# Token-mixing layer: a sixth pair of output tiles by seven products, with a sum and the residual additions done by accumulating DMAs

## The chip, the core and the metric

One Trainium2 chip, one core. Its engines run side by side, each in its own order of instructions: TensorE (PE in the profile, its weight loads PEld), VectorE (DVE), ScalarE (ACT), GpSimd (POOL) and SyncE (SP), which here only issues DMAs. POOL issues DMAs too, those that add to their destination. The metric is the device time of one execution in microseconds, lower is better; the kernel is compared by the median of its runs.

## What is computed

x is 2048 tokens by 448 channels. The first half of the layer is a linear attention block, the second a token-mixing MLP. Both add to x; six vectors (sa, ca, ga, sb, cb, gb) come from c and w_mod.

```
x = x + ga * A(layernorm(x) * (1 + ca) + sa)
h = layernorm(x) * (1 + cb) + sb
u = gelu(einsum("bsd,sf->bdf", layernorm(h), w1) + b1)     # S = 2048 -> F = 1792, across tokens
y = einsum("bdf,fs->bds", u, w2) + b2                      # F = 1792 -> S = 2048
out = x + gb * transpose(y)
```

The change lies in the last two lines: the product of u (14 row tiles of 128 by 448) with w2 (1792 by 2048), which gives 16 output tiles of 128 tokens by 448 channels, and the sum with x. The factor gb is multiplied into u, and gb * b2 is added to x beforehand (L1059).

## The kernel before, in words

**Precision.** Every 32-bit operand of a product is split into a high part that TensorE takes (written by ACT, L76) and a remainder (written by DVE, L77). A product of two split operands is three matmuls of 448 columns (`acc3`, L739 to L742): high by high, and the two mixed ones.

**Two ways to one result.** In the last stage the 16 output tiles come out of PSUM in two ways. *Plain* tiles (10 to 15 before the change): for each of 14 row tiles f of w2, `load1` fetches it, `split1` splits it, `mult1` runs three matmuls of 448 columns per output tile. One plain piece is one f, for one or two output tiles: 10 with 11, 12 with 13, then 14 and 15 alone. *Blocks* (tiles 0 to 9): two output tiles make a block q, whose part of w2 is a 2 by 2 arrangement of quarters a11, a12, a21, a22. It is multiplied by Strassen's scheme as Winograd arranged it: seven products instead of eight, of quarters or of sums of quarters. `PRODS` (L901) lists them with the sum that is made after each split: s1 = a21 + a22, s2 = s1 - a11, s3 = a11 - a21, s4 = a12 - s2. `split7` splits one factor (two pieces of 512 and 384 columns) and makes the sum with `sub` on DVE (L896). `mult7` runs one product: seven pairs of a matmul of 448 columns (L928, high part) and one of 224 (L929, remainder). The factors that come from u (`b..`, `t..`) are made once by `finish_u`.

**Out of the blocks.** `out7` runs after each product. It copies PSUM to SBUF on ACT (`copy2`, L934) and adds on DVE (`out2`: L938 of 448 columns, then two halves of 224 into x, L939 and L940; the last product adds twice straight from PSUM, L962 and L963). The finished tile of x is stored by SP (`store`, L943).

**x in between.** While w1 is being multiplied, DVE adds gb * b2 to each tile of x (L1059) and SP parks all 16 tiles in DRAM (`xpark`, L1060). The last stage fetches each back ahead of its use (`fetch_x`, L1043). The SBUF tiles of this stage all come from one pool of 76 slots; a load waits until the slot that it takes over is free.

**Order.** The order of PE's work is written out by hand: `order` is 8 plain pieces, then the products of all blocks in turn with the other plain pieces spread evenly between them, then 10 plain pieces. The loop at L1072 takes one entry at a time: loads are issued up to 12 entries ahead (`load2`, with all eight loads of a block at its first product), splits up to 4 entries ahead (`split2`), then the product and its output. Each engine runs its share of this in program order, as soon as what it waits for is there.

**The end.** For the last plain tile the last LAST = 3 pieces are held back: `mult_last` (L986) adds what is there to x, then multiplies these pieces for the first CUT = 336 columns, adds (L998) and stores (L999) them, and does the same for the other 112.

POOL issues accumulating DMAs earlier in the kernel (L244, L376, L399, L405: SBUF into SBUF), and none in this stage.

Of the kernel before, what the change touches and what calls it, by code (L numbers as in the profile page):

```python
# [8 lines left out]
F32 = mybir.dt.float32  # L9
F32R = mybir.dt.float32r  # L10
AF = mybir.ActivationFunctionType
ALU = mybir.AluOpType
AX = mybir.AxisListType

P = 128
S, D, F = 2048, 448, 1792
NT = S // P
NF = F // P
# [9 lines left out]
DVE_LOW = (0, 1, 13, 14, 15)  # L28
AHEAD = 8
LAG = 5  # L30
LAST, CUT = 3, 336
MOD_AT = {11: [(4, 0)], 12: [(4, 1)], 13: [(4, 2)], 14: [(4, 3)], 15: [(3, 0), (3, 1)]}
QS = {0: 2, 4: 2}
WARM = 12
# [10 lines left out]
def block_kernel(ctx: ExitStack, tc: tile.TileContext, x, wqkv, wo, w1, b1, w2, b2, c, wmod, out):  # L45
    nc = tc.nc
    xf = x.flatten_outer_dims()
    of = out.flatten_outer_dims()
# [4 lines left out]
    park = ctx.enter_context(tc.tile_pool(name="park", bufs=1, space=bass.MemoryType.DRAM))  # L53
# [8 lines left out]
    def slot(name, w=D, dt=F32, parts=P):  # L62
        return slots.tile([parts, w], dt, name=name, tag="slot", padded_shape=[P, 512])

    def tslot(name, dt=F32, parts=P, w=D):
        return tok.tile([parts, w], dt, name=name, tag="tok", padded_shape=[P, 512])
# [5 lines left out]
    def bank(name):  # L72
        return psum.tile([P, 512], F32, name=name, tag="bank")
# [26 lines left out]
    X = [None] * NT  # L100
# [123 lines left out]
    def load_to(i):  # L224
        while done["load"] < min(i, len(pieces)):
            k = done["load"]
            src, r, c0, n = pieces[k]
            raws[k] = slot(f"pr{k}", n * P)
            nc.sync.dma_start(raws[k], src[r * P:(r + 1) * P, c0 * P:(c0 + n) * P])
            done["load"] += 1  # L230

    def split_to(i):
        while done["split"] < min(i, len(pieces)):
            k = done["split"]
            n = pieces[k][3]
            if k in TOKP:
                hi, lo = tslot(f"ph{k}", F32R, w=n * P), tslot(f"pl{k}", F32R, w=n * P)
            else:
                hi, lo = slot(f"ph{k}", n * P, F32R), slot(f"pl{k}", n * P, F32R)
            if k in PIECE_DMA:  # L240
                full = raws.pop(k)
                nc.scalar.activation(hi, full, AF.Copy)
                nc.scalar.activation(lo, hi.bitcast(F32), AF.Copy, scale=-1.0)
                nc.gpsimd.dma_start(lo, full, accum_op=ALU.add)  # L244
            else:
                split(raws.pop(k), hi, lo)
            parts[k] = (hi, lo)
            done["split"] += 1
# [287 lines left out]
    for t in range(3, NT):  # L536
# [38 lines left out]
        if t == 4:  # L575
            for g in range(4):
                w = tslot(f"wo{g}", parts=G)
# [48 lines left out]
    for ch in range(4):  # L626
        for g in range(4):
            s = slice(g * G, (g + 1) * G)
# [133 lines left out]
    for i in range(NT + LAG):  # L762
# [13 lines left out]
        t = i - LAG  # L776
# [54 lines left out]
    uparts = ctx.enter_context(tc.tile_pool(name="uparts", bufs=1, reuse_waits="tile"))  # L831
    HD = D // 2
    PAIRS, RS = NF // 2, ((0, 4), (4, 3))
    NS7 = 5
    uw, uops, ufull = {}, {}, {}

    def u_parts(r, name, src):
# [39 lines left out]


    w2v = w2.rearrange("(r e p) c -> e p r c", e=2, p=P)
    raw2, hilo, acc2, cop = {}, {}, {}, {}  # L880
    QUADS = {"a11": (0, 0), "a12": (1, 0), "a21": (0, 1), "a22": (1, 1)}

    def load_quads(q):
        for name, (fo, to) in QUADS.items():
            raw2[q, name] = []
            for r0, n in RS:
# [2 lines left out]
                nc.sync.dma_start(w.rearrange("p (r c) -> p r c", c=P), w2v[fo, :, r0:r0 + n, c0:c0 + P])  # L889
                raw2[q, name].append(w)  # L890

    def sub(q, out, a, b, op=ALU.subtract, into=None):
        res = []
        for i, (r0, n) in enumerate(RS):
            w = raw2[q, into][i] if into else slot(f"{out}_{q}_{r0}", n * P)
            nc.vector.tensor_tensor(w, raw2[q, a][i], raw2[q, b][i], op=op)  # L896
            res.append(w)
        raw2[q, out] = res


    PRODS = (("a11", "b11", 0, ("s1", "a21", "a22", ALU.add)), ("a12", "b21", 1, ("s2", "s1", "a11")),  # L901
             ("s2", "t2", 0, ("s3", "a11", "a21", ALU.subtract, "a21")),
             ("s1", "t1", 2, ("s4", "a12", "s2", ALU.subtract, "a12")), ("s3", "t3", 0, None),
             ("s4", "b22", 2, None), ("a22", "t4", 0, None))

    def split7(q, m):
        a, _, _, add = PRODS[m]
        hilo[q, m] = []
        for w, (r0, nr) in zip(raw2[q, a], RS):
            h, l = slot(f"{a}h_{q}_{r0}", nr * P, F32R), slot(f"{a}l_{q}_{r0}", nr * P, F32R)  # L910
            split(w, h, l)
            hilo[q, m].append((h, l))
        if add:
            sub(q, *add)

    def mult7(q, m):
        a, b, k, _ = PRODS[m]
        opens = m in (0, 1, 3)
        if opens:
            acc2[q, k] = bank(f"y{q}_{k}")  # L920
        ps = acc2[q, k]
        closes = m in (1, 5, 6)
        cut = hilo.pop((q, m))
        for r in range(PAIRS):
            (h, l), i = cut[r // 4], r % 4
            w, wh = uops[b, r]
            s = slice(i * P, (i + 1) * P)
            nc.tensor.matmul(ps[:, :D], h[:, s], w, start=opens and r == 0, stop=False, skip_group_check=True)  # L928
            nc.tensor.matmul(ps[:, :HD], l[:, s], wh, start=False, stop=closes and r == PAIRS - 1,  # L929
                             skip_group_check=True)  # L930

    def copy2(q, k, name):
        cop[q, name] = slot(f"c{name}_{q}")
        nc.scalar.activation(cop[q, name], acc2[q, k][:, :D], AF.Copy)  # L934

    def out2(q, k, name, t, half):
        c, x = cop.pop((q, name)), X[t][:, half * HD:(half + 1) * HD]
        nc.vector.tensor_add(c, acc2[q, k][:, :D], c)  # L938
        nc.vector.tensor_add(x, x, c[:, :HD])  # L939
        nc.vector.tensor_add(x, x, c[:, HD:])  # L940

    def store(t):
        nc.sync.dma_start(of[t * P:(t + 1) * P, :], X[t])  # L943

    def out7(q, m):
        t0, t1 = 2 * q, 2 * q + 1
        if m == 0:
            copy2(q, 0, "c1")
        elif m == 1:
            out2(q, 1, "c1", t0, 0)  # L950
        elif m == 2:
            copy2(q, 0, "c2")
        elif m == 3:
            copy2(q, 2, "c5")
        elif m == 4:
            out2(q, 0, "c5", t1, 1)
        elif m == 5:
            out2(q, 2, "c2", t0, 1)
            store(t0)
        else:  # L960
            x = X[t1][:, :HD]
            nc.vector.tensor_add(x, acc2[q, 0][:, :HD], x)  # L962
            nc.vector.tensor_add(x, acc2[q, 0][:, HD:D], x)  # L963
            store(t1)


    def load1(t, n, f):
# [39 lines left out]


    sevens = [(q, m) for q in range(NS7) for m in range(7)]
    plains = [(t, n, f) for t, n in ((10, 2), (12, 2), (14, 1), (15, 1)) for f in range(NF)]  # L1010
    LEAD, TAIL = 8, 10
    order = [("p", p) for p in plains[:LEAD]]
    mid = plains[LEAD:len(plains) - TAIL]
# [21 lines left out]
    k = NT  # L1035
    jobs = [j for f in range(4) for j in finish_u(f, accs[f])]

    xleft = list(range(NT))
    xpark = [park.tile([P, D], F32, name=f"xpark{t}") for t in range(NT)]

    def fetch_x(t):
        X[t] = slot(f"xb{t}")
        nc.sync.dma_start(X[t], xpark[t])  # L1043

    k += LAG - 1
    for o0, n in W1G[1:]:
        if early:
            accs, first = early, LAG - 1
            early = None
        else:  # L1050
            accs, first = [bank(f"up{o0 + i}") for i in range(n)], 0
        for r in range(first, NT):
            load_to(k + AHEAD)
            split_to(k + 3)
            if jobs:
                jobs.pop(0)()
            if xleft and k % 2:
                t = xleft.pop(0)
                nc.vector.scalar_tensor_tensor(X[t], mods[5], b2c[:, t:t + 1], X[t], op0=ALU.mult, op1=ALU.add)  # L1059
                nc.sync.dma_start(xpark[t], X[t])  # L1060
                X[t] = None
            step(k, accs, H2h[r], H2l[r], r == 0, r == NT - 1)
            k += 1
            if k == len(pieces) - 8:
                load2(4)
            if k == len(pieces) - 3:
                load2(LOAD2)
                split2(2)
        jobs += [j for i in range(n) for j in finish_u(o0 + i, accs[i])]


    for n, (kind, p) in enumerate(order):  # L1072
        if jobs:
            jobs.pop(0)()
        while xleft:
            t = xleft.pop(0)
            nc.vector.scalar_tensor_tensor(X[t], mods[5], b2c[:, t:t + 1], X[t], op0=ALU.mult, op1=ALU.add)
        if kind == "s":
            if p[1] == 0:
                for t in (2 * p[0], 2 * p[0] + 1):  # L1080
                    if X[t] is None:
                        fetch_x(t)
        elif p[2] == 2:
            for t in range(p[0], p[0] + p[1]):
                if X[t] is None:
                    fetch_x(t)
        load2(n + LOAD2)
        split2(n + SPLIT2)
        if n < len(order) - LAST:
            (mult7 if kind == "s" else mult1)(*p)  # L1090
            (out7 if kind == "s" else out1)(*p)
# [27 lines left out]
```

## Time and profile before

| | |
|---|---|
| runs shown | 453.23, 453.87, 454.25 us: median 453.87 |
| profiled execution | 452.57 us, span from first to last instruction 450.8 us |
| granted TensorE clock | 1.000 |
| HBM read and written | 45.09 MB, 7.34 MB |
| DMA landing, median from issue | quarters of w2 4.9 (256 KB) and 5.1 (192 KB); x fetched back 3.9; output tile 2.0 |
| stage of the change | 319.46 us (first plain matmul of w2) to the end |

The profile is of one execution. Busy time of an engine is the time in which it worked, and a group's mean is that of one instruction; successive instructions overlap at their ends, so the distance between two starts is shorter than one duration. A line L is one of the kernel file; a helper such as `split` or `acc3` gives its line to all that call it, and the tile names tell them apart: `up` is the product with w1, `yp` a plain output, `y` a block's, `yl` the split end. "Landing" counts from the issue of a DMA to the time its data is there.

### The profile page before, as it was taken

What the parts mean: (1) busy time and instruction counts of PE and PEld (TensorE: products, weight loads), DVE (VectorE), ACT (ScalarE), POOL (GpSimd) and SP (SyncE); (2) the same over time, 40 slices, a digit from 0 to 9 for tenths busy, and PEclk for the clock granted to TensorE, in tenths of its full rate; (3) what the DMA queues carried; (4) which work ended last, traced back from release to release, by engine and by line L of the source; (5) the groups of instructions that cost most, each with busy time, mean ns of one, the idle gap of its engine ahead of it and who ended that gap; (6) DMA issues with size and microseconds to landing.
All of it is one profiled execution on the core that took longest, in us unless ns stands there. A gap on an engine that the chain in (4) does not pass through costs nothing.

```text
span 450.8 us, 7295 instructions
## 1 busy us (share of the span) xinstructions
PE 446.0 (99%) x2385; PEld 411.0 (91%) x2385; DVE 356.0 (79%) x774; ACT 250.1 (55%) x559; POOL 89.0 (20%) x162
## 2 busy tenths in 40 slices
PE   9999999999999999999999999999999999999997
PEld 8689999989899999999999999999999999999997
DVE  5797787888899899896469677539696978798993
ACT  2659877755656576767675345236546262536350
POOL 2124675620014345554300000000000000000000
PEclk9999999999999999999999999999999999999999
DMA  8949899985200003222407463417960674628313
GB/s 216 308 113 205 148 188 248 223 203 163 72 0 2 23 25 104 62 49 48 138 28 242 135 203 100 132 36 233 279 184 24 197 224 125 168 100 254 111 58 100
DMA packets 60551, 61.64 MB, mean 137 GB/s; under 512 B 9376, under 2 KB 53856, under 8 KB 60512
## 3 DMA queue, kind: packets, MB, share of 16 engines
q1 hardware_dynamic: 54896, 52.45, 39.1%
q0 software_dynamic: 5616, 8.72, 11.8%
q8 instruction: 19, 0.31, 0.3%
q14 instruction: 20, 0.16, 0.1%
HBM read 45.09 MB, written 7.34 MB: 116 GB/s over the span
## 4 chain that ended last, share of the span: by engine, by line
PE 92%; POOL 3%; issue 3%; DVE 1%; ACT 0%; POOLq 0%; DVEq 0%
PE y L928 11%; PE up L742 10%; PE up L741 10%; PE up L740 10%; PE op L689 9%; PE qp L333 7%; PE y L929 6%; PE kp L333 4%; PE cacc L420 4%; PE yp L740 4%; PE yp L742 4%; PE yp L741 4%; PE warm L141 2%; PE tq L673 2%; POOL rs L289 1%
## 5 line engine op out<-in xcount | busy, mean ns | idle before, releaser
L742 PE MATMUL up<-h2h,pl 128*128 128x448 f32 x224 | 81.4, 363 | 0.0
L741 PE MATMUL up<-h2l,ph 128*128 128x448 f32 x224 | 81.2, 363 | 0.0
L740 PE MATMUL up<-h2h,ph 128*128 128x448 f32 x224 | 80.8, 361 | 0.0
L77 DVE TENSOR_TENSOR pl<-pr,ph 128x512 fp32r<-128x512 f32 (+1 forms) x60 | 36.2, 614 | 11.1 <-ACT ph L76 7.8
L741 PEld LDWEIGHTS up<-h2l,ph 128*128 128x128 f32 x224 | 42.1, 188 | 3.1
L740 PEld LDWEIGHTS up<-h2h,ph 128*128 128x128 f32 x224 | 41.9, 187 | 3.0
L742 PEld LDWEIGHTS up<-h2h,pl 128*128 128x128 f32 x224 | 42.0, 188 | 2.4
L76 ACT ACTIVATE ph<-pr 128x512 fp32r<-128x512 f32 (+1 forms) x60 | 32.7, 569 | 12.9 <-PE up L741 11.1
L934 ACT ACTIVATE cc<-y 128x448 f32<-128x448 f32 x15 | 8.2, 545 | 56.1 <-PE y L929 47.9
L740 PE MATMUL yp<-uw,qw 128*128 128x448 f32 x81 | 29.8, 367 | 0.0
L742 PE MATMUL yp<-uw,qw 128*128 128x448 f32 x81 | 29.4, 363 | 0.0
L741 PE MATMUL yp<-uw,qw 128*128 128x448 f32 x81 | 29.4, 363 | 0.0
L689 PE MATMUL op<-wph,pth 112*128 112x448 f32 x64 | 24.5, 383 | 0.0
L420 PE MATMUL cacc<-pkh,xh 128*128 128x448 f32 x64 | 24.3, 379 | 0.0
L76 ACT ACTIVATE qw<-q 128x256 fp32r<-128x256 f32 (+1 forms) x56 | 18.9, 353 | 8.0 <-DMA q<-in_B_w_dram 7.5
L689 PE MATMUL op<-wpl,pth 112*128 112x448 f32 x64 | 23.2, 363 | 0.0
L689 PE MATMUL op<-wph,ptl 112*128 112x448 f32 x64 | 23.2, 362 | 0.0
L420 PE MATMUL cacc<-pkl,xh 128*128 128x448 f32 x64 | 23.2, 362 | 0.0
L333 PE MATMUL kp<-wh,hl 128*128 128x448 f32 x60 | 21.6, 365 | 0.6 <-DVE hl L77 0.6
L77 DVE TENSOR_TENSOR qw<-q,qw 128x256 fp32r<-128x256 f32 (+1 forms) x56 | 18.8, 350 | 3.8 <-ACT qw L76 3.8
L333 PE MATMUL kp<-wh,hh 128*128 128x448 f32 x60 | 21.6, 366 | 0.0
L333 PE MATMUL qp<-wh,hh 128*128 128x448 f32 x60 | 21.6, 366 | 0.0
(214 smaller groups left out, 1233.2 us busy)
## 6 DMA issues: line engine op xcount, KB each, us to landing
pr<-in_B_w_dram SPq DMA_DIRECT2D x48, 256.0 KB, 3.0
a<-in_B_w_dram SPq DMA_DIRECT2D x20, 256.0 KB, 4.9
wm<-in_w_mod_dram SPq DMA_DIRECT2D x24, 196.0 KB, 4.9
a<-in_B_w_dram SPq DMA_DIRECT2D x20, 192.0 KB, 5.1
x<-in_A_x_dram SPq DMA_DIRECT2D x16, 224.0 KB, 4.5
xpark<-x SPq DMA_DIRECT2D x16, 224.0 KB, 1.9
q<-in_B_w_dram SPq DMA_DIRECT2D x28, 128.0 KB, 3.5
xb<-xpark SPq DMA_DIRECT2D x16, 224.0 KB, 3.9
```

Source lines behind the costliest of these rows:

```text
L76: nc.scalar.activation(hi, full, AF.Copy)
L77: nc.vector.tensor_sub(lo, full, hi.bitcast(F32))
L141: nc.tensor.matmul(warm[:, :P], ones, ones, start=True, stop=True)
L333: nc.tensor.matmul(o, a[:, ch * P:(ch + 1) * P], b, start=(n == 0), stop=(n == 10))
L420: nc.tensor.matmul(cacc[ch][:, :D], a[:, s], b, start=(t == 0 and i == 0), stop=(t == NT - 1 and i == len(todo) - 1))
L673: nc.tensor.transpose(tps[t][:G, g * P:(g + 1) * P], pn[:, g * G:(g + 1) * G], ident)
L689: nc.tensor.matmul(opb[t][:, :D], a[:, s], b, start=(n == 0), stop=(n == 11))
L740: nc.tensor.matmul(ps[:, :D], hi[:, sl], mh, start=first, stop=False)
L741: nc.tensor.matmul(ps[:, :D], hi[:, sl], ml, start=False, stop=False)
L742: nc.tensor.matmul(ps[:, :D], lo[:, sl], mh, start=False, stop=last)
L928: nc.tensor.matmul(ps[:, :D], h[:, s], w, start=opens and r == 0, stop=False, skip_group_check=True)
L929: nc.tensor.matmul(ps[:, :HD], l[:, s], wh, start=False, stop=closes and r == PAIRS - 1, skip_group_check=True)
```

## The change

It does four things. Tiles 10 and 11 become a sixth block (NS7 = 6), so blocks give 12 tiles and plain pieces 4. The sum s1 = a21 + a22 is no longer made on DVE: after a block's loads, POOL issues two DMAs that add a22 to a21 in place; s3 is made as a22 - s2, which is the same, and is put in a11's place. For the 12 tiles of the blocks x is written to the output itself instead of to the park; nothing is fetched back, and `out2` adds the two halves of a product's result into a new tile `yt`, which a POOL DMA adds to the output in DRAM (`add_to_x`). The last product goes through an ACT copy and one DVE add. One-column memsets on DVE (`await_x`) wait for the stores of x, so that nothing is added to the output before x is there. And the tail is cut otherwise: LAST = 2, CUT = 224.

```diff
-LAST, CUT = 3, 336
+LAST, CUT = 2, 224
-    NS7 = 5
+    NS7 = 6
...
     def load_quads(q):
...
+        raw2[q, "s1"] = raw2.pop((q, "a21"))
+        for w, a in zip(raw2[q, "s1"], raw2[q, "a22"]):
+            nc.gpsimd.dma_start(w, a, accum_op=ALU.add)
...
-    PRODS = (("a11", "b11", 0, ("s1", "a21", "a22", ALU.add)), ("a12", "b21", 1, ("s2", "s1", "a11")),
-             ("s2", "t2", 0, ("s3", "a11", "a21", ALU.subtract, "a21")),
+    PRODS = (("a11", "b11", 0, None), ("a12", "b21", 1, ("s2", "s1", "a11")),
+             ("s2", "t2", 0, ("s3", "a22", "s2", ALU.subtract, "a11")),
...
     def out2(q, k, name, t, half):
-        c, x = cop.pop((q, name)), X[t][:, half * HD:(half + 1) * HD]
+        c = cop.pop((q, name))
         nc.vector.tensor_add(c, acc2[q, k][:, :D], c)
-        nc.vector.tensor_add(x, x, c[:, :HD])
-        nc.vector.tensor_add(x, x, c[:, HD:])
+        nc.vector.tensor_add(yt(t)[:, half * HD:(half + 1) * HD], c[:, :HD], c[:, HD:])
+
+    def add_to_x(t):
+        nc.gpsimd.dma_start(of[t * P:(t + 1) * P, :], ysum.pop(t), accum_op=ALU.add)
...
-            store(t0)
+            add_to_x(t0)
         else:
-            x = X[t1][:, :HD]
-            nc.vector.tensor_add(x, acc2[q, 0][:, :HD], x)
-            nc.vector.tensor_add(x, acc2[q, 0][:, HD:D], x)
-            store(t1)
+            y = yt(t1)[:, :HD]
+            nc.scalar.activation(y, acc2[q, 0][:, :HD], AF.Copy)
+            nc.vector.tensor_add(y, acc2[q, 0][:, HD:D], y)
+            add_to_x(t1)
...
-    plains = [(t, n, f) for t, n in ((10, 2), (12, 2), (14, 1), (15, 1)) for f in range(NF)]
+    plains = [(t, n, f) for t, n in ((12, 2), (14, 1), (15, 1)) for f in range(NF)]
...
-    xpark = [park.tile([P, D], F32, name=f"xpark{t}") for t in range(NT)]
+    xpark = {t: park.tile([P, D], F32, name=f"xpark{t}") for t in range(2 * NS7, NT)}
+    stored = []
+
+    def put_x(t):
+        if t in xpark:
+            nc.sync.dma_start(xpark[t], X[t])
+        else:
+            nc.sync.dma_start(of[t * P:(t + 1) * P, :], X[t])
+            stored.append(X[t])
+        X[t] = None
+
+    def await_x(n):
+        while len(stored) > n:
+            nc.vector.memset(stored.pop(0)[:, 0:1], 0.0)
...
-                nc.sync.dma_start(xpark[t], X[t])
-                X[t] = None
+                put_x(t)
+                await_x(3)
...
-        if kind == "s":
-            if p[1] == 0:
-                for t in (2 * p[0], 2 * p[0] + 1):
-                    if X[t] is None:
-                        fetch_x(t)
-        elif p[2] == 2:
+        await_x(0)
+        if kind == "p" and p[2] == 2:
```

## The prediction

> **What bounds the kernel now.** I read the busy shares first, then the slices and the chain, then the PE timeline of the last stage.
>
> ```profile
> PE 446.0 (99%) x2385; PEld 411.0 (91%) x2385; DVE 356.0 (79%) x774; ACT 250.1 (55%) x559; POOL 89.0 (20%) x162
> PE   9999999999999999999999999999999999999997
> PE 92%; POOL 3%; issue 3%; DVE 1%; ACT 0%; POOLq 0%; DVEq 0%
> ```
>
> TensorE (PE) is busy in 99% of the span, in every slice but the last, and is 92% of the chain. So a microsecond counts if it is PE's, or lies behind PE's last matmul, or if it makes PE wait. The stage that the change touches, from the first `yp` matmul (319.46) to the split tail (445.46), has no gap on PE:
>
> ```profile
> 329.06:445.46 116.40, 116.40 (x687) 109.92 (x685) 97.20 (x215) 51.43 (x127) 0.00 (x0) 1.00 0.48 142
> ```
>
> Columns are length, then busy time of PE, weight loads, DVE, ACT and POOL, then the granted clock (1.00), the DMA share and GB/s. DVE works 97.2 of 116.4 us, ACT 51, POOL nothing.
>
> **What one more block is worth.** The price of a matmul is the distance between starts, since the profile's durations overlap:
>
> ```profile
> 361.25 0.27 PE L929 MATMUL y<-ut,s2l 128*128 128x224 f32 x1
> 361.35 0.37 PE L928 MATMUL y<-ut,s2h 128*128 128x448 f32 x1
> 361.56 0.26 PE L929 MATMUL y<-ut,s2l 128*128 128x224 f32 x1
> 361.66 0.38 PE L928 MATMUL y<-ut,s2h 128*128 128x448 f32 x1
> ...
> 362.19 0.36 PE L741 MATMUL yp<-uw,qw 128*128 128x448 f32 x1
> 362.39 0.36 PE L742 MATMUL yp<-uw,qw 128*128 128x448 f32 x1
> 362.59 0.36 PE L740 MATMUL yp<-uw,qw 128*128 128x448 f32 x1
> ```
>
> A plain matmul of 448 columns takes 0.200 us. Two plain tiles are 2 x 14 x 3 = 84 of them: 16.80. A block does the same two tiles in 49 pairs of a 448 and a 224. To price a pair with its transitions I take the whole stretch: 319.46 to 445.46 is 126.0 us, it holds 81 x 3 = 243 plain matmuls (48.6), and the rest, 77.4, is 5 blocks of 15.48 (0.316 a pair; the fourth block, 400.70 to 420.98 less 24 plain matmuls, gives the same). Tiles 10 and 11 turn from plain into a block: **16.80 - 15.48 = -1.32 us** on PE. The plain pieces that stand between the sevens only move.
>
> The Trainium skill (TensorE: Matmul & The Clock Gate, Back-to-back issue gap) gives N/2.4 + 2.5 ns between warm starts. By an estimate from that page the pair would be 189 + 96 ns, the block 13.96, two plain tiles 15.89, and the gain 1.93; the rows here are 200 and 316 ns, so I sum with the rows.
>
> **The tail.** LAST 3 -> 2 and CUT 336 -> 224. Now:
>
> ```profile
> 445.46 2.48 PE L995 MATMUL yl<-uw,qw 128*128 128x336 f32 x18
> 447.04 0.51 DVE L998 TENSOR_TENSOR xb<-yl,xb 128x336 f32<-128x336 f32 x1 [0.75 <-PE yl L995]
> 447.98 0.27 DVE L998 TENSOR_TENSOR xb<-yl,xb 128x112 f32<-128x112 f32 x1 [0.44 <-PE yl L995]
> 448.28 0.34 SPq L999 DMA_DIRECT2D out_dram<-xb  x1
> ```
>
> The nine of 336 columns start 0.153 apart, the nine of 112 0.11 apart, although they have a third of the columns. A 224 costs 0.105 to 0.11 (above), so halves are cheaper: 3 plain matmuls (0.60) and twelve 224s (the last starts at 0.60 + 11 x 0.11 = 1.81 and takes 0.27) end 2.08 after 445.46, against 2.48 now. Behind them: 0.04, an add of 224 columns from PSUM (0.39, rows of L962 and L963, now 0.27), 0.03 to the store's issue: 2.54 against 2.82. The last store is 112 KB; the trace has 1.53 us to landing for 56 KB and 1.82 for 168 KB, I take 1.65. Tail: -0.28 + 0.12 = **-0.16**.
>
> **DVE, ACT, SP.** By pitch (1.07 us for the two parts of a split or sum, 0.65 and 0.31 to 0.43 for the adds) DVE pays 16.8 us per block now: 7 splits 7.5, 4 sums 4.3, three outputs of 1.4, 0.8 for the last. The change takes one sum and four 224-column adds: 7.5 + 3.2 + 3 x 0.96 + 0.31 = 13.9. A block with its four plain pieces is 15.48 + 2.4 = 17.9 us of PE in the later blocks, where DVE then has 14.8, so DVE is relieved, worth nothing while PE has no gap. ACT gains a copy of 224 columns per block (below 0.55, the row of 448), on an engine that works 51 of 116. The twelve memsets of one column wait for stores that landed in 1.9 us and were issued three turns (some 14 us) before. On SP, 12 stores to DRAM remain (other address), 12 fetches of x and 12 of the late output stores go. These stores hold SP's queue now (24.7 us of waits for L940's adds), so later loads start no later. Each is costed at nothing; the cover is PE's unbroken queue.
>
> **Where the cover could break: the sum by DMA.** s1 = a21 + a22 leaves DVE (1.07 us) and becomes two POOL DMAs per block. Behind them waits DVE's s2 = s1 - a11, and behind that, in order, all of DVE. Rows for such a DMA:
>
> ```profile
> pl<-pr POOLq DMA_DIRECT2D x4, 256.0 KB, 4.3
> pk<-pk POOLq DMA_DIRECT2D x12, 224.0 KB, 4.6
> ```
>
> Their single landings reach 6.63 us; issuing takes POOL 0.86 to 1.3. First block: a22's two parts landed at 320.86 and 321.39. The second accumulation is issued at 321.9 and lands at 326.2, or at 328.5 by the slowest row. Now the order on DVE:
>
> ```profile
> 327.36 1.15 DVE L896 TENSOR_TENSOR s<-a,a 128x512 f32<-128x512 f32 x2
> 328.43 0.69 DVE L77 TENSOR_TENSOR ut<-tb,ut 128x224 fp32r<-128x224 f32 x2
> ...
> 330.44 1.15 DVE L896 TENSOR_TENSOR s<-s,a 128x512 f32<-128x512 f32 x2
> ```
>
> Without s1 and with one plain split less ahead (0.33), s2 starts at about 329.0: the DMA is there, 0.5 us early at worst. PE wants s2's split at 334.7 (one plain piece fewer before it than now, 335.91); from s2's start DVE and ACT need 3.3, so PE waits only if the sum lands after 331.4. Later blocks: the program's order puts the accumulations of block q+1 on POOL behind the two output additions of block q-1. From the end of that block's last product: 1.1 to its `yt`, three issues of 0.9, landing 4.3 to 6.6, is 8.1 to 10.4; DVE reaches s2 of block q+1 when PE starts the last product of block q, 17.9 - 2.2 = 15.7 after. Five us are left. Bounds of this step: 0 and, with a landing 12 us instead of 4.3, some +3; I take 0, by the nearest rows.
>
> **The additions to the output.** 12 POOL DMAs of 224 KB. No row adds into DRAM. Nearest: 1.95 us to land a store of that size, 4.2 to 6.6 for the accumulating rows into SBUF. Eleven have time. The last goes out behind the last product, whose end I call X. Program order: nine plain pieces (5.4), twelve 224s (1.32 with 0.16 drain) and the end as above put the last store's landing at X + 9.0. The addition: drain 0.2, ACT copy 0.4, DVE add 0.4, issue at X + 1.1, landing at X + 3.1 to X + 7.7. It is covered up to a landing time of 7.9 us. The Trainium skill (DMA: Bandwidth & Descriptors, Anatomy of one DMA) has 2.0 us + bytes/436e3 per DMA of this path, by estimate 2.5 us here, and says that the receipt is slowest where the target is HBM; the SBUF rows are already near twice that. By its figure this step would be 0 too.
>
> **Sum:** -1.32 - 0.16 = -1.48. The profiled execution took 452.57 (span 450.8), so 451.1 on its base; it lay 1.30 under the median 453.87, so **452.4** as a median (-0.33%).
>
> **Rivals.**
> 1. *Slower: additions into DRAM are slow.* Place: the last `yt`, behind PE's end. For it: no row shows this target, and reading DRAM costs more than writing it (fetch of x 3.9, store 2.0). Against: 7.9 us of cover. Each us beyond is a us of time: at 9.4 us the gain is gone, from 10.3 on it is slower by over 0.2%, at 12 us 452.4 + 4.1 = 456.5. Later q loads also wait for a `yt` slot then. 6%.
> 2. *s1 late, DVE stalls, PE starves.* Price worked out above: landing 331.4 is the point; 3 us more is 455.4. For: the DMA share is 0.89 around 320 to 329, when these run. Against: 2.9 us of room over the slowest row. 5%.
> 3. *No change: the gain leaks out at the block borders.* From the end of (q,5) DVE does its output (0.96), then a11 of the next block (1.07): 2.1, and PE needs it 3.4 after (0.6 + 2.2 + 0.6). 1.3 us is the narrowest place; 0.3 lost in each of five borders would leave 453.9. Now the same place holds with DVE's longer outputs. 8%.
> 4. *A larger gain, pairs nearer to columns/2.4:* 1.93 instead of 1.32, 451.8. The rows hold in five blocks, so 3%. (This is what the pitch of the Trainium skill, TensorE: Matmul & The Clock Gate, Back-to-back issue gap, would lead to.)
>
> The forecast has 78%, in it 72% by over 0.2% and 6% within it (0.2%, 0.9 us, is about what a measurement of this kernel can tell from no change). Faster: 72 + 3 + 2 of rival 1 with small lateness = 77%. Within: 6 + 6 of rival 3 + 1 = 13%. Slower: 10%. Range: 451.5 (rival 4 and the spread of the runs, 453.23 to 454.25) to 453.9 (rival 3, small lateness).
>
> **What would show it.** Right: PE without gaps from 319 to its end, 245 + 49 pairs 0.316 apart, the stage 1.3 shorter, L896's group of s1 gone from DVE, no DVE wait for a DMA at s2, the last `out_dram<-yt` landed before the last `out_dram<-xb`. Wrong: PE idle before `s2h` products with DVE waiting for a DMA named a; the chain's end on `yt`; landings of `out_dram<-yt` over 8 us; `q` or `a` loads that land later than now with ACT waiting for them.

## The result and the profile after

The changed kernel takes **451.94 us** (median of 11 runs, 451.50 to 452.91); the kernel before, on the same chip, 453.23 (452.55 to 454.25). The ratio is 0.9976, 95% interval 0.9966 to 0.9985: 0.24% faster, or 1.1 us with 0.7 to 1.5 as its bounds (the two medians lie 1.29 apart). 452.4 had been forecast from a median of 453.87, that is -0.33%.

From the page of the changed kernel, the busy shares, the queue of POOL's DMAs (packets, MB, share of the DMA engines) and the chain:

```profile
PE 444.3 (98%) x2396; PEld 408.5 (91%) x2396; DVE 352.0 (78%) x767; ACT 255.7 (57%) x568; POOL 109.0 (24%) x186
...
q0 software_dynamic: 9072, 14.23, 19.9%
...
PE 86%; POOL 4%; issue 4%; DVE 2%; DMA 1%; SPq 1%; ACT 0%; POOLq 0%; DVEq 0%
```

PE has 1.7 us less to do, DVE 4, ACT 5.6 more, POOL 20 more. The last stage up to the split tail still has no gap on PE; by windows of the same length as the one shown of before:

```profile
329.78:446.18 116.40, 116.40 (x706) 109.97 (x705) 93.25 (x197) 57.07 (x137) 19.39 (x22) 1.00 0.65 144
```

DVE fell from 97.2 to 93.25 us, POOL rose from nothing to 19.39, PE's column equals the length as before. So what PE has to do still sets the time.

The profiled execution took 452.91 us (span 451.1), which is more than the 452.57 of before. That is no contradiction: the difference arose ahead of this stage. The first `yp` matmul starts at 320.72 instead of 319.46, behind instructions of PE that stand in the same order in both. The waits of PE before 320 us (in total, times, longest) are, before:

```profile
PE kp L333 <- DVE hl L77: 0.6, 1, 0.6
```

and after:

```profile
PE kp L333 <- DVE hl L77: 1.1, 2, 0.8
...
PE tp L312 <- DVE h L300: 0.4, 1, 0.4
PE modp L177 <- DMA wm<-in_w_mod_dram: 0.3, 1, 0.3
```

In thirteen profiled executions, of kernels that are alike or nearly so up to there, the first `yp` matmul started anywhere from 318.71 to 320.72. The place at which PE loses this early time changes from execution to execution; in these two all the waits lie before 205 us, and the first thing that the change does, a store of x, is at 236. So I count from the first `yp` matmul, at which the changed stage begins, and leave totals to the medians:

| from the first `yp` matmul, us | before | after | difference |
|---|---|---|---|
| to the first matmul of the split tail | 126.00 | 125.46 | -0.54 |
| to PE's end | 128.48 | 126.95 | -1.53 |
| to the last store's landing | 130.35 | 129.07 | -1.28 |
| from that landing to the span's end | 0.96 | 1.34 | +0.38 |

(The first line holds 243 plain matmuls before and 162 after, since two tiles became a block and the tail takes two pieces instead of three.) The last line was not in my sum: SP ends with a row of nine waits on semaphores, 0.06 us apart, the same in both kernels. What differs is the place in this row of the semaphore that the last store releases: before, it is the eighth of the nine, so two waits are left when the store has landed; after, it is the second, and eight are left. Six more waits are 0.38 us. What remains is -0.90 us, inside the interval of the medians.

The tail after, to be read beside that of before (start, duration, engine):

```profile
446.18 1.49 PE L1007 MATMUL yl<-uw,qw 128*128 128x224 f32 x12
...
447.11 0.39 DVE L1010 TENSOR_TENSOR xb<-yl,xb 128x224 f32<-128x224 f32 x1
447.53 0.94 SPq L1011 DMA_DIRECT2D out_dram<-xb  x2
447.71 0.39 DVE L1010 TENSOR_TENSOR xb<-yl,xb 128x224 f32<-128x224 f32 x1 [0.21 <-PE yl L1007]
```

Two equal halves: twelve matmuls in 1.49 us, the add of 0.39, the store. It landed at 449.79, 1.66 after its issue. The last addition to the output was issued at 442.14 and landed at 446.08, so the store ends the kernel.

The narrow spot is the first block's sum by DMA. DVE's rows of s2:

```profile
330.30 0.68 DVE L900 TENSOR_TENSOR s<-a,a 128x512 f32<-128x512 f32 x1
332.01 0.56 DVE L900 TENSOR_TENSOR s<-a,a 128x384 f32<-128x384 f32 x1 [1.03 <-DMA a<-a]
```

DVE stood for 1.03 us until the second accumulation landed (331.99). And the landings of these DMAs in the stretch 320 to 334 (KB, median us from issue):

```profile
a<-a POOLq DMA_DIRECT2D x1, 256.0 KB, 7.3
...
a<-a POOLq DMA_DIRECT2D x1, 192.0 KB, 8.5
```

That is slower than the slowest row that I had (6.63). The quarters that SP loads at the same time land in up to 8.5 us too. So the sign that I had named, no wait of DVE for a DMA at s2, did not hold. PE did not notice: s2's split was done at 333.98, 2.0 us before PE reached its product at 336.00.

### The profile page after: what moved, and what is told of

It reads as the page before. It is cut to its first block, busy times and chain, and to the rows that moved or that the text cites. A ratio compares the mean times of both kernels' runs of the same rounds, so it can differ in the third digit from the quotient of the medians.

```text
span 451.1 us, 7324 instructions
## 1 busy us (share of the span) xinstructions
PE 444.3 (98%) x2396; PEld 408.5 (91%) x2396; DVE 352.0 (78%) x767; ACT 255.7 (57%) x568; POOL 109.0 (24%) x186
## 4 chain that ended last, share of the span: by engine, by line
PE 86%; POOL 4%; issue 4%; DVE 2%; DMA 1%; SPq 1%; ACT 0%; POOLq 0%; DVEq 0%
PE y L932 14%; PE up L742 10%; PE up L741 10%; PE up L740 10%; PE op L689 9%; PE qp L333 7%; PE y L933 7%; PE cacc L420 3%; PE kp L333 3%; PE yp L740 2%; PE yp L742 2%; PE yp L741 2%; PE tq L673 2%; POOL xl L376 1%; DMA wm<-in_w_mod_dram 1%
## 5 line engine op out<-in xcount | busy, mean ns | idle before, releaser
L894 POOL DMA_DIRECT2D a<-a x12 | 11.2, 1070 | 110.3 <-PE yp L742 97.0
L952 POOL DMA_DIRECT2D out_dram<-yt x12 | 10.5, 873 | 85.7 <-DVE yt L943 57.3
L938 ACT ACTIVATE cc<-y 128x448 f32<-128x448 f32 x18 | 9.8, 544 | 23.3 <-PE y L933 23.3
L333 PE MATMUL qp<-wh,hl 128*128 128x448 f32 x60 | 21.4, 363 | 0.0
L677 ACT ACTIVATE pth<-tq 112x512 fp32r<-112x512 f32 x16 | 9.6, 599 | 20.5 <-PE tq L673 17.7
L289 POOL TENSOR_TENSOR rs<-ve,mhalf 128x1 f32<-128x1 f32 x16 | 14.3, 896 | 24.5 <-DVE ve L287 23.9
```

Of the source, the lines that this page charges most:

```text
L289: nc.gpsimd.tensor_tensor(rs, ve, mhalf[:, 0:1], op=ALU.pow)
L333: nc.tensor.matmul(o, a[:, ch * P:(ch + 1) * P], b, start=(n == 0), stop=(n == 10))
L894: nc.gpsimd.dma_start(w, a, accum_op=ALU.add)
```

## The experiments

All were timed beside the kernel before, in three groups (its medians: 452.82, 452.42 and 452.75). "Stage" runs from the first `yp` matmul to the first of the split tail, in the profiled execution; stages compare where the plain matmuls are equally many.

| | ratio to before | 95% interval | stage, us | plain matmuls in it |
|---|---|---|---|---|
| changed kernel | 0.9976 | 0.9966 to 0.9985 | 125.46 | 162 |
| five blocks | 1.0011 | 0.9999 to 1.0024 | 126.60 | 246 |
| sum on DVE | 0.9975 | 0.9967 to 0.9984 | 125.46 | 162 |
| outputs by DVE | 1.0018 | 1.0007 to 1.0029 | 126.77 | 162 |
| six blocks alone | 0.9986 | 0.9976 to 0.9996 | 125.79 | 162 |
| stores off SP | 0.9986 | 0.9971 to 1.0001 | 125.46 | 162 |
| late sum | 1.0371 | 1.0342 to 1.0399 | 140.40 | 162 |
| late sum, own tiles | 1.0197 | 1.0175 to 1.0220 | 133.80 | 162 |
| short tail | 1.0021 | 1.0012 to 1.0030 | 125.47 | 162 |
| seven blocks | 0.9943 | 0.9931 to 0.9955 | 123.85 | 78 |
| seven, sum on DVE | 0.9967 | 0.9953 to 0.9982 | 124.47 | 78 |
| seven, no DMA sums | 1.0125 | 1.0108 to 1.0142 | 132.11 | 78 |

### Which part makes the gain

My theory was that the sixth block makes nearly all of it and that the DMA parts only give engines air. The rival: the relief of DVE by the DMA additions makes it. Four kernels take the change apart.

**Five blocks**: the changed kernel without the sixth block.

```diff
-    NS7 = 6
+    NS7 = 5
-    plains = [(t, n, f) for t, n in ((12, 2), (14, 1), (15, 1)) for f in range(NF)]
+    plains = [(t, n, f) for t, n in ((10, 2), (12, 2), (14, 1), (15, 1)) for f in range(NF)]
```

> The changed kernel with five blocks again (tiles 10 and 11 plain), all its DMA additions and the new tail kept. Theory (the gain is PE time of one block, 16.80 - 15.48 = 1.32 us, and nothing else counts because PE has no gap): stage from the first yp matmul to the split tail about 126.6 us (125.46 + 1.32 less what the tail's piece shifts), time 1.1 to 1.5 us over the changed kernel, so within 0.4 us of the kernel before. Rival (the relief of DVE and SP by the DMAs is part of the gain): time clearly below the kernel before, by 0.6 us or more.

Measured: 1.0011. Stage 126.60, as expected, without a gap on PE:

```profile
319.63:446.23 126.60, 126.60 (x738) 119.49 (x736) 93.86 (x209) 59.67 (x152) 17.56 (x20) 1.00 0.64 152
```

With all the rest of the change in place the gain is gone. The same profile gives the tail by itself: PE's end 0.39 earlier than before (128.09 from the first `yp` matmul), the last landing 0.13 earlier (130.22). From here to the changed kernel, where only the sixth block is added, both are 1.14 to 1.15 less. That this kernel is no faster than the one before, in spite of its tail, fits its end: 1.64 us pass from the last landing to the span's end, against 0.96 before.

**Sum on DVE**: the changed kernel with s1 made by DVE again, in a21's place.

```diff
-        raw2[q, "s1"] = raw2.pop((q, "a21"))
-        for w, a in zip(raw2[q, "s1"], raw2[q, "a22"]):
-            nc.gpsimd.dma_start(w, a, accum_op=ALU.add)
-    PRODS = (("a11", "b11", 0, None), ("a12", "b21", 1, ("s2", "s1", "a11")),
+    PRODS = (("a11", "b11", 0, ("s1", "a21", "a22", ALU.add, "a21")), ("a12", "b21", 1, ("s2", "s1", "a11")),
```

> The changed kernel with s1 = a21 + a22 made on DVE again (in a21's place), six blocks and the output additions by DMA kept. Theory (the sum by DMA is hidden either way): PE without gaps, DVE about 6.4 us busier, time within 0.4 us of the changed kernel, ratio to the kernel before 0.997. The wait of DVE for the accumulation in the first block (1.03 us) is gone and changes nothing. Rival (DVE needs this relief at a block of 17.9 us): PE gaps ahead of s3h or s4h products, 0.2 us or more per block, 1 us or more in all.

Measured: 0.9975, stage 125.46, both those of the changed kernel. With six blocks the sum by DMA is worth nothing.

**Outputs by DVE**: the kernel before with six blocks, the new tail and s1 by DMA, but the old adds into x, park, fetch and stores.

> Six blocks, the new tail and s1 by DMA, but the outputs as before: x parked and fetched back, four adds of 224 columns more per block on DVE, stores by SP. DVE by pitch 15.7 + 0.8 of 17.9 us per block. Theory: PE still without gaps, ratio 0.997. Rival 1 (DVE's order): outputs stand ahead of splits, PE waits at the block borders, 0.3 us per block, time about 1.5 us more. Rival 2 (SP's order): SP's stores and fetches stand ahead of the loads of the next block, the accumulation that follows them lands late, DVE waits for it and PE behind it, 1 us or more in one block or in several.

**Six blocks alone**: the same without the sum by DMA, so no accumulating DMA in this stage at all. Only `LAST, CUT`, `NS7` and `plains` differ from the kernel before.

> The kernel before with six blocks and the new tail, none of the DMA additions. DVE by pitch 16.8 + 0.8 = 17.6 of the 17.9 us that PE needs per block. Theory (only PE's work counts): ratio 0.997 like the changed kernel, gain 1.3 us. Rival (the DMA additions are what makes the sixth block possible): by adding up DVE's order from the end of one block's sixth product, s3's split ends some 0.2 us after PE wants it, so PE loses 0.2 to 0.5 us per block, 1 to 2.5 us, ratio 0.999 to 1.003, with gaps ahead of the s3h products.

Measured: 0.9986 for the six blocks alone, with one gap (0.33 us ahead of and within s3's product in the last block, at 433); 1.0018 with the sum by DMA added to that, with gaps of 0.18 us at 414.5, 0.27 at 427.6 and 0.87 at 432.4 to 433.5. The theory of both had been 0.997, and both miss it. For the six blocks alone the rival's place was right, but its price of 0.2 to 0.5 us per block was paid once only. So the sum by DMA *costs* 0.3% if the outputs stay as they were, although it takes a microsecond per block from DVE. That was no part of my prediction (rival 2 of this run's expectation had named it), and the trace shows the way. DVE's and SP's waits in this kernel:

```profile
DVE s L900 <- DMA a<-a: 5.2, 5, 1.3
```

```profile
SPq L947 <- DVE xb L944: 29.5, 5, 12.3
SPq L947 <- DVE qw L77: 20.2, 5, 4.9
```

SP stands for 50 us in the stores of finished tiles (L947), which wait for DVE's adds, and the loads of the next quarters are queued behind them. The accumulations wait for these loads: those of the fifth and sixth block went out at 401.44 and 419.80, in the changed kernel at 390.12 and 408.03. DVE, in its order, then waits at s2 for the landing. The next kernel tests this.

**Stores off SP**: the outputs by DVE as above, but POOL issues the stores of the blocks' tiles.

```diff
     def store(t):
-        nc.sync.dma_start(of[t * P:(t + 1) * P, :], X[t])
+        (nc.gpsimd if t < 2 * NS7 else nc.sync).dma_start(of[t * P:(t + 1) * P, :], X[t])
```

> The kernel with six blocks and s1 by DMA but the old way of the outputs (adds into x on DVE, park, fetch), which was 1.0018 of the kernel before, with one change: the stores of the blocks' tiles are issued by POOL instead of SP. DVE's work is the same. Theory (there the accumulating DMAs came late because SP's queue holds stores that wait for DVE, and the loads of a behind them): with SP relieved the accumulations of the fifth and sixth block are issued about 10 us earlier, DVE no longer waits for a<-a, PE's gaps at 414, 427 and 432 go, ratio 0.997 to 0.999. Rival (it is DVE's load that starves PE, or the fetches of x, not the stores): the gaps stay and the ratio is 1.001 to 1.003.

Measured: 0.9986, and a stage of 125.46 without a gap, that of the changed kernel to the hundredth; the accumulations go out at 390.27 and 408.18. DVE's wait is down to one:

```profile
DVE s L900 <- DMA a<-a: 0.6, 1, 0.6
```

DVE does as much work as in the kernel with the gaps (111.97 us against 111.88 between 319 and 449). So it was the queue, not DVE's load. It also says what the additions to the output did for this kernel: they took the waiting stores off SP.

### How much room the sum by DMA has

**Late sum**: POOL copies a22 first and then adds the copy, so that s1 comes later.

```diff
-        for w, a in zip(raw2[q, "s1"], raw2[q, "a22"]):
-            nc.gpsimd.dma_start(w, a, accum_op=ALU.add)
+        for i, (w, a) in enumerate(zip(raw2[q, "s1"], raw2[q, "a22"])):
+            c = slot(f"ac_{q}_{i}", RS[i][1] * P)
+            nc.gpsimd.dma_start(c, a)
+            nc.gpsimd.dma_start(w, c, accum_op=ALU.add)
```

> The changed kernel, but each sum s1 = a21 + a22 goes by two DMAs one behind the other: POOL first copies a22 into a free tile, and when that has landed adds the copy to a21. The result is the same, only later by one landing (4 to 8 us). Theory (the sum by DMA costs nothing because it lands ahead of its use, and in the first block only just): in the changed kernel's profile the first block's second addition landed at 331.99 and s2's split was done 2.1 us before PE wanted it, while the later blocks had 7 to 13 us. A landing 4 to 7 us later uses up the first block's 2.1 us and leaves the later blocks whole: PE stands idle for 1.5 to 4.5 us once, ahead of the first s2 product, and nowhere else; ratio to the kernel before 1.001 to 1.008, stage from the first yp matmul to the split tail 127 to 130 us instead of 125.46. Rival (the deadline is softer than worked out, or POOL's waiting delays the additions to the output and the later blocks starve too): no gap and a ratio near 0.9976, or gaps ahead of s2 in several blocks and a ratio over 1.01.

Measured: 1.0371, stage 140.40: far more than expected. The first block did what was worked out: the second addition landed at 334.70 and PE stood for 2.2 us at 333.5. But there were three more stalls of 1.5 to 4.7 us and one of 0.7, and ACT's waits show one that does not belong to the sum:

```profile
ACT qw L76 <- DMA a<-ac: 8.0, 2, 5.1
```

A plain piece's split does not read `ac`. I took it for the slot: the copies pass through the common pool, and a later split was given a copy's slot.

**Late sum, own tiles**: the copies get two tiles of a pool of their own.

> The late sum again (POOL copies a22, then adds the copy to a21), but the copies have two tiles of their own instead of slots of the common pool. In the first try the first block behaved as worked out (second addition landed at 334.70, DVE's second s2 part right after it, PE without work for 2.2 us once), but three later blocks stood for 1.5 to 4.7 us each with ACT's split of a plain piece or of a quarter waiting for a<-ac, which it does not read: theory, its slot had been a copy's. Then with tiles of their own only the first block's 2.2 to 2.5 us are left, the stage is 127.6 to 128.0, the ratio to the kernel before 1.001 to 1.004. Rival: the later stalls come from POOL's order (waits for loads and landings in front of the additions to the output) or from sums that are really late there; then the ratio stays above 1.015.

Measured: 1.0197, stage 133.80. The later stalls shrank from 1.5 to 4.7 us to two of 0.9 and 0.5 us and two pauses of 0.3, so most of them had been slots, but the expected 2.2 to 2.5 in the first block became 4.6, because its second addition landed at 337.30 here. My "later by one landing" was wrong: POOL issues in order, the first addition waits for the first copy, and the second copy stands behind it; the second half comes two landings later. That holds in the first late kernel as well (first copy landed at 326.05, second copy and second addition at 331.28 and 334.70), so its agreement with one landing was luck. It holds in the later blocks too, where DVE waited for `a<-ac` (15.1 us in five waits).

Together the two give the deadline. Counted from the first `yp` matmul, the second half of the first block's sum landed at 15.45 and PE lost 2.0 us; at 18.08 it lost 4.6; in the changed kernel it landed at 11.27 and PE lost nothing. Landing less loss is 13.4 and 13.5: PE starves from there on, a microsecond for each microsecond, and the changed kernel had 2.2 us left in this execution. In the five other kernels whose first block makes the sum in the same way the second half landed at 8.0 to 11.5, which leaves 2.0 to 5.4.

The stall also had an aftermath. Windows of the second late kernel: the stall, the 4 us behind it, the time after (granted clock in the third column from the end):

```profile
333.00:338.50 5.50, 1.08 (x7) 0.68 (x6) 1.87 (x4) 1.15 (x3) 1.45 (x2) 1.00 0.44 108
338.50:342.50 4.00, 4.00 (x15) 3.66 (x15) 4.00 (x9) 2.60 (x6) 1.42 (x2) 0.57 0.52 115
342.50:396.50 54.00, 54.00 (x330) 51.02 (x330) 41.53 (x84) 25.69 (x59) 10.96 (x14) 1.00 0.76 188
```

For 4 us PE was granted 0.57 of its clock on average (half of it from 338.85 to 342.26, 3.41 us), and its matmuls lost another 1.65 us against their usual pitch. Behind the 4.7 us stall of the first late kernel it was 1.65 us as well. In these two cases the stall cost a third more than it lasted.

### The cover of the last addition

**Short tail**: the changed kernel with `TAIL = 2` instead of 10, so that eight plain pieces move from behind the last block to between the products.

> The changed kernel with TAIL = 2 instead of 10: eight of the plain pieces that stand behind the last block are spread between the blocks' products, so that only one whole piece and the split end are left behind the last product. PE's work is the same. Theory (the additions to the output are free only because later plain work covers the last one): in the changed kernel the last addition was issued 1.42 us after the last product's end, landed 3.94 later, and the last store 3.7 after that. Without the eight pieces (4.9 us) the store lands 4.2 us after the last product, the addition at 5.3 to 8.4: the end of the program moves to the addition, +1.1 us at a landing of 3.9 and up to +4.1 at the slowest one of 6.9; ratio 1.000 to 1.007, and the chain of waits ends on yt. Rival (a DMA that adds is not a matter of the end at all, or the pieces between the products help PE as much): the ratio stays at 0.9976 within 0.1%.

Measured: 1.0021, slower than before. By the ratios it is some 2.0 us slower than the changed kernel; the profile shows 1.36 of it: the last landing is 130.43 from the first `yp` matmul instead of 129.07. The size is within the theory's range, the way is not the theory's. The addition landed 5.19 us after the last product, as worked out (5.3), and the chain does not end on it. Instead the last two stores, which ran beside it, were slow. Their landings (min, median, max) with the short tail:

```profile
DMA to landing us min/median/max: 3.0/3.2/3.3
```

and in the changed kernel:

```profile
DMA to landing us min/median/max: 1.7/1.7/1.7
```

So the end moved before the addition was the last thing itself. That the addition is what slowed the stores is not shown: it is one profile, and no run here puts as much plain traffic beside the last stores. Elsewhere the rows point both ways: in the six blocks alone two stores of 224 KB beside plain loads, at 362 us, took 3.7 us instead of the usual 1.95, and in the changed kernel one beside an addition, at 425.6, took 2.0.

### What the DMA parts buy: seven blocks

If DVE's work per block is what the DMA parts buy, they must begin to matter where a block leaves DVE less time. With a seventh block (tiles 12 and 13) no plain piece is left between the products, and a block has 15.5 us instead of 17.9.

**Seven blocks**: the changed kernel, with tiles 14 and 15 as one plain pair ahead of the blocks and behind them.

```diff
-    NS7 = 6
+    NS7 = 7
-    plains = [(t, n, f) for t, n in ((12, 2), (14, 1), (15, 1)) for f in range(NF)]
-    LEAD, TAIL = 8, 10
+    plains = [(14, 2, f) for f in range(12)] + [(t, 1, f) for t in (14, 15) for f in (12, 13)]
+    LEAD, TAIL = 8, 8
...
-                 f == NF - 1 - (LAST if t == NT - 1 else 0))
+                 f == NF - 1 - (LAST if t + i == NT - 1 else 0))
```

> The changed kernel with a seventh block (tiles 12 and 13), and the remaining tiles 14 and 15 as one plain pair: eight pieces of both ahead of the blocks, four behind them, then the last two pieces of each as before. Between the products of the blocks no plain piece is left. Theory (a block is worth 16.80 - 15.51 = 1.29 us as long as PE has no gap): stage shorter by another 1.3 us, ratio 0.9940 to 0.9955, if DVE (13.9 us per block, of 15.5) keeps up. Rival (the border of the blocks, the narrowest place: without plain pieces DVE has 15.5 us per block instead of 17.9): PE waits in front of a11 or s2 products at several borders, 0.3 us or more each, and the ratio is 0.996 to 1.000.

Measured: **0.9943** (0.9931 to 0.9955), faster than both kernels. PE has no gap in the stage:

```profile
319.18:443.03 123.85, 123.85 (x765) 117.36 (x764) 107.20 (x218) 68.61 (x148) 24.66 (x28) 1.00 0.72 153
```

The blocks take (123.85 - 78 x 0.2) / 7 = 15.46 us each.

**Seven, sum on DVE**: this kernel with s1 on DVE, by the edit shown above.

> Seven blocks with s1 made on DVE again (into a21), the additions to the output still by DMA. Theory (a sum by DMA is worth what DVE lacks, and nothing else): DVE's work per block is 13.9 + 1.07 = 15.0 us of the block's 15.5, so it still holds: within 0.15% of the seven blocks with the sum by DMA (0.9943), that is 0.993 to 0.996. Rival (at the narrow border of two blocks the 1.07 us more come too late, there being no plain piece between): a gap of 0.3 to 1 us in each of six borders, ratio 0.998 to 1.006.

Measured: 0.9967, stage 124.47: one gap, ahead of a22's product, the last of the first block (0.57 us from start to start instead of 0.10). Between the theory (0.993 to 0.996) and the rival (0.998 to 1.006); 0.62 us of the 1.1 by which the ratio is higher are seen in the profile, and the two intervals just touch, so that the sum by DMA is worth 0.24% here is likely, not certain.

**Seven, no DMA sums**: seven blocks and the new tail on the kernel before, with s1 and the outputs on DVE.

> Seven blocks and the new tail with nothing done by accumulating DMAs: s1 on DVE, outputs added into x on DVE, park, fetch and SP's stores as in the kernel before. Theory (the two DMA parts buy DVE time, which decides as soon as a block has less than DVE's 16.8 us): 1.3 us are lacking in each 15.5 us block; over seven blocks, less the lead that DVE has at the start, PE loses 4 to 9 us: ratio 1.003 to 1.015, gaps ahead of s2, s3 or a11 products in most blocks with DVE busy throughout. Rival (DVE's durations by pitch overstate its work, it keeps up): 0.994 to 0.998.

Measured: 1.0125, stage 132.11, in which PE works 125.53 and DVE 124.25. There are six gaps of 1.1 to 2.2 us, 8.3 us against the seven blocks with DMA. All six stand at the same place, ahead of a22's product, the last of a block:

```profile
376.50 0.62 DVE L938 TENSOR_TENSOR cc<-y,cc 128x448 f32<-128x448 f32 x1
377.15 0.39 DVE L939 TENSOR_TENSOR xb<-xb,cc 128x224 f32<-128x224 f32 x1
377.18 0.47 PE L928 MATMUL y<-ut,a22h 128*128 128x448 f32 x1 [0.93 <-DVE cc L938]
```

That product adds into the bank that DVE's add of the fifth product (L938) has still to read, and DVE comes to it only after the splits and sums of the next block that stand ahead of it.

So the change's DMA parts bring about 0.1% at six blocks (0.9986 to 0.9976, intervals overlapping; 0.33 us by the stages) and 1.8% at seven (1.0125 to 0.9943).

## Why the prediction was right, point by point

- **The sixth block, -1.32 us.** Right in kind, too large by 0.18: -1.14 from five blocks to six. The mis-sized term is the block: 15.51 us instead of 15.48, and that in all six blocks. The pair's two starts are 0.2128 and 0.1019 us apart after, 0.2113 and 0.1021 before. The step that was a little off is "The plain pieces that stand between the sevens only move": there are also fewer of them between products, 24 instead of 38, so more products (18 of 42) follow directly on another one, and such a product is slower. a12's product takes 2.240 us behind another product (all six blocks after) and 2.210 behind a plain piece (all five blocks before); the short tail has both orders in one kernel, with these same two times. It is not the DMA traffic: the five blocks, with all the DMAs, have the pair of before (0.2113 and 0.1021), and the six blocks alone, with no accumulating DMA, have about that of after (0.2131 and 0.1023, their one gap included). With seven blocks the pair is 0.2137 and 0.1019; the 15.46 is lower only because the plain matmuls next to a product, which cost about 0.02 us more at each change, are hardly there any longer. Why a product behind a product is slower stays open.
- **The tail, -0.16 us.** Measured by the five blocks: PE's end -0.39 (worked out: -0.40), the last landing -0.13. Right.
- **The program's last waits.** Missing from the sum: +0.38 us behind the last landing, by the place of the last store's semaphore in SP's row of waits. It is not a price of the additions: the six blocks alone, which have none, have 1.33 us there, and the seven blocks without DMA sums 0.96.
- **The base.** I set the sum against 453.87, a median of three; over eleven runs the kernel before is at 453.23. That is why the time came out below the forecast though the gain was smaller; that it came within 0.5 us of 452.4 is in part luck.
- **Relief of DVE, ACT and SP worth nothing.** Right for DVE at this size: with s1 back on DVE nothing changes. Of SP I had only said that later loads start no later. In truth its relief is what the sum by DMA needs: without it that sum costs 0.3%.
- **The sum by DMA, 0 us, room in the first block.** Right by two errors that partly cancelled. Counted from the first `yp` matmul I had the landing at 6.7, at the latest 9.0; it was 11.27, since beside the loads such a DMA took 8.5 us (5.3 to 8.5 over the six kernels that have it). I had the deadline at 11.9; it was 13.4 to 13.5: PE wanted s2 when I had worked it out (15.3), but from the last half's landing DVE and ACT needed 2.0 us, not 3.3 from s2's start. The room was 2.2 us in this execution, not 2.9 over the slowest case. The later blocks had 7.8 to 12.7 us, more than the five worked out.
- **The additions to the output, 0 us.** Right. Landings of 3.87 to 6.94 us, median 4.2, inside the bounds of 2.0 to 6.6 but for the slowest; the last 3.94. The store landed at X + 9.07 (worked out: 9.0), the addition at X + 5.36. The Trainium skill (DMA: Bandwidth & Descriptors, Anatomy of one DMA) had led to 2.5 us by estimate; every landing was longer, and the rows from SBUF to SBUF (4.3 to 4.6) were the better guide.
- **Rival 1** did not happen; with its cover taken away (the short tail) the end did move, but by stores that landed late beside the addition, not by the addition. **Rival 2** did not happen either; in the two late kernels, where the sum does come too late, it has the place and the price named (a microsecond for each), with a later deadline. **Rival 3** did not happen, and named the wrong spot: where DVE was short with seven blocks, PE stopped ahead of a22's product for a bank, and with six blocks alone at s3's, not at a11's. **Rival 4** fell: the blocks cost 15.46 to 15.51, not less.

## What to carry to other kernels

Where one engine has no gap, price a change by that engine's pitch alone, in the order in which its instructions will stand (here a product right behind another one is slower), and treat what relieves the others as room: ask at which size the room will be needed, and try that size, for there the change may be worth far more (here a seventh block). When a sum moves from an engine to a DMA, look first at the queue that feeds it: waiting stores ahead of its loads turned the same edit from free into 0.3%. A kernel's early part can vary by more than the change is worth, so compare profiles from the first instruction of the changed stage on, and totals by medians.

## What the runs showed of the hardware that I had not expected

- **Accumulating DMAs beside loads.** Within SBUF, in the first block (DMA share 0.9 and more), 256 KB landed in 4.7 to 7.3 us and 192 KB in 5.3 to 8.5, over six kernels; later on in 3.0 to 5.9 (7.4 once, in the seven blocks). With DRAM as the target 224 KB took 3.87 to 6.94 us in the changed kernel, median 4.2, and up to 8.3 in the five blocks.
- **Stores beside an accumulating DMA.** In one execution 112 KB landed in 3.0 to 3.3 us instead of 1.66, at a DMA share of about 0.8. Whether it is the adding or just the traffic is open.
- **The clock after a stall.** After a stall of 4.8 us PE was granted 0.57 of its clock over 4 us, half of it for 3.41. The Trainium skill (TensorE: Matmul & The Clock Gate, What's actually happening) has half the clock after an idle window of about 3.4 us, which agrees. But in the first late kernel a stall of 2.6 us, which began 0.5 us after one of 0.7 had ended, was followed by half the clock from 371.66 to 375.07 (0.62 between 372 and 376 us), so a shorter one can do it; single stalls of 2.2 us left the clock at 1.00 (at 333.5 in the first late kernel, at 409.4 in the seven blocks without DMA sums).
- **The end of the program.** From the last landing to the span's end: 0.96 to 1.64 us, mostly by where the last store's semaphore stands in SP's row of nine waits of 0.06 us.
- **A product behind a product.** The same fourteen matmuls of a12 take 2.240 us behind another product and 2.210 behind a plain piece.
